# A quadratic for part of the exponentials, a tighter guard, a factor moved into a copy, and a new order

## The chip, the cores and the metric

The kernel runs on one core of one Trainium2 chip. The core has five engines that work side by side: TensorE (PE, matrix products; its weight loads are shown as PEld), ScalarE (ACT, activations), VectorE (DVE), GpSimd (POOL) and SyncE (SP, which issues most of the DMAs). The metric is the time of one execution on the device in microseconds (us). A version is judged by the median of several runs.

## The reference

Two attention blocks with 32 heads of 32 columns each work on separate inputs of 2048 rows and 1024 columns, in bfloat16, and their outputs are joined. A is plain softmax attention over all 2048 keys. B is cut into four segments of 512 rows: in each there is causal softmax attention within the segment, mixed through a gate `g` with what a memory of the earlier segments answers.

```python
# A
qkv = (x @ wqkv).reshape(B, S, 3, H, Dh).transpose(2, 0, 3, 1, 4)
scores = einsum('bhqd,bhkd->bhqk', q, k) * Dh ** -0.5
o = einsum('bhqk,bhkd->bhqd', softmax(scores), v)
a = o.transpose(0, 2, 1, 3).reshape(B, S, D) @ wo
# B
phi = lambda t: where(t > 0, t + 1.0, exp(t))
g = sigmoid(beta).reshape(1, H, 1, 1)
for s in range(4):
    p = softmax(einsum('bhqd,bhkd->bhqk', qs, ks) * Dh ** -0.5 + mask)
    a_dot = einsum('bhqk,bhkd->bhqd', p, vs)
    a_mem = (phi(qs) @ M) / (phi(qs) @ z + 1e-6)
    outs.append(g * a_mem + (1.0 - g) * a_dot)
    M, z = M + phi(ks).T @ vs, z + sum(phi(ks))
b = concat(outs) @ wo
return concat([a, b], axis=-1)
```

The logits are small: from the reference's inputs, the largest product of A is 0.042 after scaling.

## The kernel before

**Units, sets, tiles.** The heads are taken in eight groups of four (`g` in A, `j` in B). A unit of A is one group and 256 query rows, 64 units in all; a unit of B is two groups of one segment. A set is 256 query rows against two blocks of 128 keys for four heads: four tiles of 128 x 512, one for each head. A whole unit of A is eight sets. For each set TensorE writes the scores into four banks of PSUM (line 915), ScalarE takes their exponential in two instructions of 1024 columns into the ring `P` of 20 tiles (L994), and TensorE multiplies the result with the values and with a column of ones, for the sum of the row (L1090 and L1097, "P·V" in what follows; an accumulator in one PSUM bank). At the end of a unit, `recip_rows` transposes the sums (L1115), copies the values out of the bank (`keep`, L1118), takes the reciprocal (L1125), in B multiplies it by 1-g (L1127), and transposes back (L1129); GpSimd multiplies the values by it (L1175 to L1195).

**Polynomial tiles.** The table `CUBIC` gives for every four units of A which sets hand the tile of their first head to a polynomial instead of ScalarE: 118 sets, whose first exponential is 512 columns wide instead of 1024. VectorE scales the scores into `Y` (L952), GpSimd adds a constant (L955) and multiplies (L956) into `Z`, and VectorE finishes with (Z + b)·Y into `Pc` (L957). `Y` has three buffers, `Z` and `Pc` two each.

**The guard.** The polynomial, and an exponential without a bias, hold for small logits. So for each group GpSimd squares K and Q (L1266, `sqA`, `sqB`), TensorE sums the squares (L1275), VectorE takes the maxima (L1282), spreads them with TensorE's help (`dg` L1319, then L1328, L1336), and writes a bias and a flag (L1342 to L1353): the flag is set when half the sum of the largest squared norms, scaled, is over `FREE`. Before the first exponential of a group ScalarE waits for the flag, loads it and branches to a second copy of its program, with biases, where the flag is set. There the polynomial tiles are done anew by ScalarE; the instruction that would do so, the carrier, is an exponential `CARRY` half-sets later, and P·V on the tile waits for its carrier in either copy.

**Projections** (L556: K, Q and V of later groups, output projections, the memory) are jobs that share bank 6: TensorE fills it, VectorE copies it out (L1248).

**The order** is made by a planner before the program is built. Every instruction has an assumed duration (in `dve`, `act`, `pool`: elements / rate / 1000 + fixed, in us) and a key, its place on a planned time axis that advances by 1.024/1.2 + 0.051 for each full exponential. A simulated run then picks for each engine what goes next. For TensorE, scores go when the exponentials are about to need them; the rest by rank, the lowest first: P·V by how many exponentials its tile is behind (`PV_ROOM`, `PV_T`), a job by how far its key lies ahead (`JOB_AT`, `JOB_SLOPE`) and by its due time (`DUE_AT`, `DUE_SLOPE`), with `STICK` taken off for staying in the same mode. `LEAD_A` is how long before its group's first exponential a group's K, Q and guard are due. Each engine then executes its list strictly in that order, with semaphore waits, and DMAs are issued from SP's list in the same manner.

The lines around the rank, which the change reaches through its constants:

```python
def rank(x):
    if x.pvn is not None:
        k = (x.pvn + PV_ROOM - st["opn"]) * PV_T if st["rows"] and x.need - st["opn"] > PV_HOT else -100.0
    else:
        k = JOB_AT + JOB_SLOPE * max(min(x.key - st["prog"], 20.0), -20.0)
        k = min(k, DUE_AT + DUE_SLOPE * (x.due - st["prog"]))
    if x.mode == mode:
        k -= STICK
```

## Time and profile before

| | |
|---|---|
| runs | 1124.29, 1128.17, 1129.32 us; median 1128.17 |
| profiled execution | span 1128.2 us |
| DMA | 72.77 MB, 64 GB/s on the mean |
| TensorE clock granted | 0.996 on the mean |

Busy time of the engines in five stretches, us:

| stretch, us | PE | DVE | ACT | POOL |
|---|---|---|---|---|
| 0 to 50 | 43.40 | 17.15 | 33.33 | 10.40 |
| 200 to 250 | 47.59 | 33.95 | 48.64 | 34.22 |
| 400 to 450 | 43.57 | 44.64 | 48.40 | 36.46 |
| 900 to 950 | 42.13 | 35.64 | 41.26 | 34.96 |
| 1050 to 1100 | 49.34 | 24.50 | 49.81 | 20.78 |

A group of instructions is shown as: line, engine, operation, output <- input, shapes, count | busy us, mean ns of one | idle time of the engine ahead of them, and what ended most of it. A wait is shown as: engine, line <- what released it: us in total, times, longest. A row of the timeline gives start, duration, engine, line, and in brackets the idle time before. Waits at a branch and DMA issues are not counted as busy. Releasers are inferred from semaphore events.

### The profile page before, as it was taken

To read this page: it belongs to the slowest core of one execution; us is meant where nothing else is said; L and a number is where in the kernel's file an instruction comes from. 1 tells how busy PE (TensorE), PEld (TensorE's weight loads), DVE (VectorE), ACT (ScalarE), POOL (GpSimd) and SP (SyncE) were. 2 spreads that over 40 slices of the span, in tenths; PEclk is the share of its full clock that TensorE was granted. 3 is DMA by queue.
4 is the path that set the end of the run, shared out by engine and by line. 5 is a ranking of instruction groups with operands and counts; after the bars stand their busy time and mean duration, and the time that the engine had idled before them with its cause. 6 is when DMAs were issued, how large, how long until landed. Compare 5 with 4: busy or idle time off the path is not lost.

```text
span 1128.2 us, 67476 instructions
## 1 busy us (share of the span) xinstructions
PE 1045.6 (93%) x31412; PEld 724.2 (64%) x31412; DVE 744.9 (66%) x1566; ACT 1071.5 (95%) x1224; POOL 677.5 (60%) x653
## 2 busy tenths in 40 slices
PE   8989999999999988998999898988999889999998
PEld 4667666667666655666666566766667556657775
DVE  3345667756665588777865888687745868775444
ACT  4989999999999999999999999999999979999997
POOL 2215576756576576856565786775755758665431
PEclk9999999999999999999999999999999989999999
DMA  9032350005223240033241330133040640022101
GB/s 203 7 85 46 83 130 15 16 19 121 54 56 88 64 104 13 16 72 63 65 90 59 82 59 11 33 87 85 27 101 28 200 111 3 23 69 76 39 23 54
DMA packets 171145, 72.77 MB, mean 64 GB/s; under 512 B 134768, under 2 KB 169072, under 8 KB 170864
## 3 DMA queue, kind: packets, MB, share of 16 engines
q1 hardware_dynamic: 168496, 67.66, 24.8%
q8 instruction: 246, 4.03, 1.5%
q10 hardware_dynamic: 2368, 0.79, 0.3%
q14 instruction: 35, 0.29, 0.1%
HBM read 45.23 MB, written 11.67 MB: 50 GB/s over the span
## 4 chain that ended last, share of the span: by engine, by line
ACT 48%; PE 35%; DVE 8%; issue 4%; POOL 2%; SPq 1%; DMA 1%; ACTq 0%; DVEq 0%; POOLq 0%
ACT P L994 47%; PE ps L556 17%; PE ps L915 7%; PE ps L1090 5%; PE ps L1097 5%; DVE PKQ_B L1546 1%; DVE Y L952 1%; DVE Pc L957 1%; SPq L1232 1%; PE ps L1495 1%; POOL Z L955 1%; ACT PKQ_B L1541 1%; DVE T L1115 1%; POOL Z L956 1%; DVE rc L1127 1%
## 5 line engine op out<-in xcount | busy, mean ns | idle before, releaser
L994 ACT ACTIVATE P<-ps 128x1024 bf16<-128x1024 f32 (+1 forms) x1176 | 1043.1, 1076 | 35.0 <-PE ps L1097 12.9
L1097 PE MATMUL ps<-P,onesb 128*32 128x256 bf16 (+1 forms) x4628 | 297.7, 271 | 1.0 <-issue 1.0
L955 POOL TENSOR_SCALAR Z<-Y 128x512 f32<-128x512 f32 x118 | 182.2, 1544 | 158.1 <-DVE Y L952 157.5
L1090 PE MATMUL ps<-P,V_A 128*32 128x256 bf16 x3860 | 254.9, 275 | 6.1 <-ACT P L994 2.1
L915 PE MATMUL ps<-KQ_A 32*128 32x256 bf16 x4096 | 205.2, 273 | 28.7 <-ACT P L994 18.9
L956 POOL TENSOR_TENSOR Z<-Z,Y 128x512 f32<-128x512 f32 x118 | 153.1, 1297 | 4.3
L915 PEld LDWEIGHTS ps<-KQ_A 32*128 32x128 bf16 x4096 | 61.9, 92 | 141.5 <-ACT P L994 100.9
L556 PE MATMUL ps<-xT_B,W_B 128*32 128x256 bf16 x4096 | 139.5, 275 | 6.1 <-issue 1.9
L556 PE MATMUL ps<-xT_A,W_A 128*32 128x256 bf16 (+1 forms) x3968 | 138.4, 277 | 5.3 <-DMA xT_A<-in_A_x_dram 1.6
L1097 PEld LDWEIGHTS ps<-P,onesb 128*32 128x32 bf16 x4628 | 130.3, 97 | 16.5 <-issue 12.1
L1014 POOL TENSOR_SCALAR_AFFINE_SELECT P<-P 128x768 bf16<-128x768 bf16 (+1 forms) x96 | 78.6, 823 | 90.7 <-ACT P L994 86.8
L1090 PEld LDWEIGHTS ps<-P,V_A 128*32 128x32 bf16 x3860 | 109.2, 96 | 32.3 <-issue 15.9
L952 DVE TENSOR_SCALAR Y<-ps 128x512 f32<-128x512 f32 x118 | 80.9, 686 | 72.3 <-PE ps L915 71.1
L1266 POOL TENSOR_TENSOR sqA<-KQ_A 128x512 bf16<-128x512 bf16 x61 | 66.6, 1094 | 96.9 <-DVE KQ_A L1248 57.2
L556 PEld LDWEIGHTS ps<-xT_B,W_B 128*32 128x32 bf16 x4096 | 100.5, 97 | 31.3 <-issue 24.1
L556 PEld LDWEIGHTS ps<-xT_A,W_A 128*32 128x32 bf16 x3968 | 97.5, 96 | 31.6 <-issue 17.0
L957 DVE SCALAR_TENSOR_TENSOR Pc<-Z,Y 128x512 bf16<-128x512 f32 x118 | 103.3, 876 | 18.9 <-POOL Z L956 18.5
L1266 POOL TENSOR_TENSOR sqB<-KQ_B 128x512 bf16<-128x512 bf16 x64 | 69.9, 1095 | 56.6 <-DVE KQ_B L1248 40.8
L1115 DVE STREAM_TRANSPOSE T<-ps 128x256 f32<-128x256 f32 (+1 forms) x148 | 71.9, 486 | 22.9 <-PE ps L1097 17.1
L1248 DVE CAST KQ_A<-ps 128x512 bf16<-128x512 f32 x60 | 41.2, 687 | 54.0 <-PE ps L556 53.7
L556 PE MATMUL ps<-Wv_B,xT_B 128*32 128x256 bf16 x2048 | 69.8, 274 | 4.8 <-DVE V_B L1248 1.4
L1129 DVE STREAM_TRANSPOSE T<-rc 128x256 f32<-128x256 f32 (+1 forms) x152 | 72.1, 478 | 2.5
(104 smaller groups left out, 1405.8 us busy)
## 6 DMA issues: line engine op xcount, KB each, us to landing
Wv_B<-in_B_wv_dram SPq DMA_DIRECT2D x32, 256.0 KB, 3.3
W_B<-in_B_wk_dram SPq DMA_DIRECT2D x32, 256.0 KB, 3.2
W_B<-in_B_wq_dram SPq DMA_DIRECT2D x32, 256.0 KB, 4.5
Wo_B<-in_B_wo_dram SPq DMA_DIRECT2D x32, 256.0 KB, 3.3
out_dram<-outsb SPq DMA_DIRECT2D x56, 128.0 KB, 1.8
W_A<-in_A_wqkv_dram SPq DMA_DIRECT2D x14, 256.0 KB, 3.6
ot_a_scratch<-OTst SPq DMA_DIRECT2D x50, 64.0 KB, 2.2
xT_A<-ot_a_scratch SPq DMA_DIRECT2D x6, 512.0 KB, 6.7
```

The costliest lines, as they stand in the source:

```text
L556: ins = e.matmul(out[r], w[:, r], x, start=start, stop=stop, tile_position=(0, 32 * t), skip_group_check=True)
L915: ins = e.matmul(out, kap, qap, start=st, stop=True, tile_position=(32 * h, 0), skip_group_check=True)
L952: o = self.dve(lambda e: e.tensor_scalar(Y[:, :], src, KAPPA * SCALE, -KAPPA * ROOT, ALU.mult, ALU.add), 512, key - 9.0, [self.bank[bank]] ...
L955: self.pool(lambda e: e.tensor_scalar(Z[:, :], Y[:, :], CUBE_A, None, ALU.add), 512, key - BCK, [rY], [rZ], rate=0.38)
L956: self.pool(lambda e: e.tensor_tensor(Z[:, :], Z[:, :], Y[:, :], ALU.mult), 512, key - BCK, [rY, rZ], [rZ], rate=0.435)
L957: last.append(self.dve(lambda e: e.scalar_tensor_tensor(out=dst, in0=Z[:, :], scalar=CUBE_B, in1=Y[:, :], op0=ALU.add, op1=ALU.mult), 512, ...
L994: a = self.act(guarded if early else lambda e: e.activation(dst, src, ACT.Exp, scale=SCALE), cols, key, rd, wr, fixed=EXP_FIXED)
L1014: self.pool(lambda e: e.affine_select(v, v, pattern=pat, compare_op=ALU.is_ge, fill=0.0, base=0, channel_multiplier=-1), 2 * nd * P, key + ...
L1090: ins = e.matmul(self.ps[32 * h:32 * h + 32, 512 * obk + q0:512 * obk + q0 + nq], v, p, start=first, stop=last, tile_position=(0, 32 * h), ...
L1097: ins = e.matmul(self.ps[32 * h:32 * h + 32, lcol + q0:lcol + q0 + nq], self.onesb[:, 0:32], p, start=False, stop=last, tile_position=(0, ...
L1115: self.dve(lambda e: e.transpose(T2[:, 0:n], src), n, nk, rsrc, [r2], fixed=0.17)
L1266: self.pool(lambda e: e.tensor_tensor(sq[:, :], src, src, ALU.mult), 512, key, [rsrc], [rs], rate=0.5)
```

## The change

The cubic in `Y` becomes a quadratic in its vertex form, C2·(y + MID)² + REST: VectorE scales and shifts, GpSimd squares (both inputs are `Y`), and GpSimd multiplies and adds into `Pc`. VectorE's last pass is gone, and P·V on `Pc` now waits for GpSimd. The guard's limit goes from 0.125 to 0.1. The factor 1-g is applied in the copy of the values instead of to the reciprocals. The code for `CHAIN`, which was 0, goes. `CUBE_PV`, `CARRY`, the last entry of `CUBIC`, the third one, and most of the planner's constants are different, so the order of all engines' lists is planned anew.

```diff
@@ -28,16 +28,17 @@
 T_RING = 3
 PHI_AT = 7.583
 EXP_FIXED = 0.051
-FREE = 0.125
+FREE = 0.1
 UP = 1.0 + 2.0 ** -7
-KAPPA, ROOT, CUBE_A, CUBE_B = 0.5501767600212002, -1.5993248390626598, -0.9857377158509045, 1.2295944671136563
-CUBIC = [[1, 3], [1, 3], [2, 4], [1, 3], [1, 3], [1, 3], [1, 3], [1, 3], [1, 3], [1, 3], [1, 3], [1, 3], [1, 3], [1, 3], [1, 3], [1, 3, 5]]
-CHAIN = 0
-CUBE_PV = 2.427
-CARRY = 7
+C0, C1, C2 = 1.00000312, 1.00124921, 0.499688252
+MID = C1 / (2.0 * C2)
+REST = C0 - C2 * MID * MID
+CUBIC = [[1, 3], [1, 3], [1, 3], [1, 3], [1, 3], [1, 3], [1, 3], [1, 3], [1, 3], [1, 3], [1, 3], [1, 3], [1, 3], [1, 3], [1, 3], [1, 4, 6]]
+CUBE_PV = 1.563
+CARRY = 5
 WHOLE = (("A", 7, 7), ("A", 7, 6))
-BCK = 8.851
-SOON = 0.388
+BCK = 6.382
+SOON = -0.051
 
 PAIR = ((6, 0), (6, 1), (6, 2), (7, 0), (7, 1), (7, 2), (6, 3), (7, 3), (6, 4), (7, 4), (6, 5), (7, 5), (6, 6), (7, 6), (6, 7),
         (7, 7))
@@ -46,8 +47,8 @@
 WARM = (15, 8)
 X_PIECES = ((0, 0, 4, 1.4, 5.0), (0, 4, 8, 4.2, 2.4), (1, 0, 4, 3.6, 3.9), (1, 4, 8, 2.9, 3.0), (2, 0, 8, 4.4, 3.0),
             (3, 0, 8, 4.9, 3.0))
-B_FIRST, B_STEP, B_GAP = 8.777, 1.325, 3.197
-B_STEP3 = 1.03
+B_FIRST, B_STEP, B_GAP = 8.777, 1.325, 3.16
+B_STEP3 = 1.029
 
 
 class Res:
@@ -148,29 +149,29 @@
 LAT = {"PE": 0.22, "ACT": 0.29, "DVE": 0.10, "POOL": 0.15, "SP": 0.1}
 SWITCH = 0.10
 WIN = 3.413
-ROW_LEAD = 0.796
+ROW_LEAD = 0.655
 AHEAD = 19.5
-HEAT = 0.666
-STICK = 2.198
+HEAT = 0.917
+STICK = 1.597
 OVER = 1.755
-PV_ROOM = 3.546
+PV_ROOM = 3.422
 PV_T = 0.844
-PV_HOT = 1.023
+PV_HOT = 1.322
 NORM_K = 8.39
-JOB_AT = -0.604
-JOB_SLOPE = 0.767
-MARGIN = 3.147
+JOB_AT = -1.233
+JOB_SLOPE = 0.629
+MARGIN = 3.142
 RXJ = 4
-RX0 = 37.688
-LEAD_A, LEAD_B, DUE_AT, DUE_SLOPE = 14.484, 8.287, 2, 1.085
+RX0 = 37.292
+LEAD_A, LEAD_B, DUE_AT, DUE_SLOPE = 16.237, 8.287, 2, 1.277
 HOLD = {}
-XR = 11.254
-XC = 0.711
+XR = 10.156
+XC = 0.833
 STEP = 1.462
-OUT3 = 55.735
+OUT3 = 55.401
 WOA_STEP = 2.224
-OUT_D = 59.313
-M_AT = 4.042
+OUT_D = 54.565
+M_AT = 5.385
 
 
 class Prog:
@@ -949,16 +950,14 @@
 
         def f(key):
             src = self.ps[:, 512 * bank:512 * bank + 512]
-            o = self.dve(lambda e: e.tensor_scalar(Y[:, :], src, KAPPA * SCALE, -KAPPA * ROOT, ALU.mult, ALU.add), 512, key - 9.0,
+            o = self.dve(lambda e: e.tensor_scalar(Y[:, :], src, SCALE, MID, ALU.mult, ALU.add), 512, key - 9.0,
                          [self.bank[bank]], [rY], fixed=0.15)
             o.urgent = True
-            self.pool(lambda e: e.tensor_scalar(Z[:, :], Y[:, :], CUBE_A, None, ALU.add), 512, key - BCK, [rY], [rZ], rate=0.38)
-            self.pool(lambda e: e.tensor_tensor(Z[:, :], Z[:, :], Y[:, :], ALU.mult), 512, key - BCK, [rY, rZ], [rZ], rate=0.435)
-            last.append(self.dve(lambda e: e.scalar_tensor_tensor(out=dst, in0=Z[:, :], scalar=CUBE_B, in1=Y[:, :], op0=ALU.add,
-                                                                  op1=ALU.mult), 512, key - BCK, [rY, rZ], [rP], fixed=0.31))
+            self.pool(lambda e: e.tensor_tensor(Z[:, :], Y[:, :], Y[:, :], ALU.mult), 512, key - BCK, [rY], [rZ], rate=0.435)
+            last.append(self.pool(lambda e: e.tensor_scalar(dst, Z[:, :], C2, REST, ALU.mult, ALU.add), 512, key - BCK, [rZ], [rP],
+                                  rate=1.1))
         self.item(T + 0.001, f)
-        return (lambda e: e.activation(dst, Y[:, :], ACT.Exp, bias=self.bias[:, 60 + bc:61 + bc], scale=1.0 / KAPPA),
-                bc, rY, rP, last, t)
+        return (lambda e: e.activation(dst, Y[:, :], ACT.Exp, bias=self.bias[:, 60 + bc:61 + bc], scale=1.0), bc, rY, rP, last, t)
 
     def plan_exp(self, take, slot, buf, T, lo=0, fix=None):
         w = take[0]["w"]
@@ -988,7 +987,7 @@
 
                 def alt(e):
 
-                    e.wait_ge(self.pg.sems["DVE"], c.count)
+                    e.wait_ge(self.pg.sems["POOL"], c.count)
                     redo(e)
                     return guarded(e)
             a = self.act(guarded if early else lambda e: e.activation(dst, src, ACT.Exp, scale=SCALE), cols, key, rd, wr,
@@ -1020,24 +1019,16 @@
 
 
         rounds = []
-        waiting = None
         for take, pv, T, cube in sets:
             at = T + 0.3
             four = list(self.sets[take[0]["set"]])
-            late = four[0] if cube else None
             for sk in {sk for sk, _ in pv}:
                 for x in self.sets[sk]:
                     x.setdefault("fixed", -1e9)
             parts = [[(x, pi) for x in self.sets[sk]] for sk, pi in pv]
-            if cube and CHAIN:
-                parts = [[(waiting, pi)] * (waiting is not None) + p[1:] for p, (_, pi) in zip(parts, pv)]
-                waiting = late
-            elif cube:
+            if cube:
                 at += CUBE_PV
             rounds.append([max([at] + [x["fixed"] + 0.001 for p in parts for x, _ in p]), take[3]["n"], parts])
-        if waiting is not None:
-            at = max(sets[-1][2] + 0.31, waiting["fixed"] + 0.001)
-            rounds.append([at, sets[-1][0][3]["n"], [[(waiting, pi)] for _, pi in pv]])
         rounds.sort(key=lambda r: r[:2])
         rest = {h: sum(x["h"] == h for r in rounds for p in r[2] for x, _ in p) for h in range(4)}
         begun = set()
@@ -1115,7 +1106,10 @@
         self.dve(lambda e: e.transpose(T2[:, 0:n], src), n, nk, rsrc, [r2], fixed=0.17)
         if keep is not None:
             rk = self.r_keep[i]
-            self.dve(lambda e: e.tensor_copy(T2[:, n:2 * n], keep), n, nk, rsrc, [rk])
+            if scale is None:
+                self.dve(lambda e: e.tensor_copy(T2[:, n:2 * n], keep), n, nk, rsrc, [rk])
+            else:
+                self.dve(lambda e: e.tensor_scalar(T2[:, n:2 * n], keep, scale, None, ALU.mult), n, nk, rsrc + [self.r_g], [rk], fixed=0.2)
         v = T2[:, 0:n].rearrange("p (b r) -> p b r", r=32)[:, :, 0:1]
         rv = rc[:, 0:nb].unsqueeze(2)
         if add is not None:
@@ -1123,8 +1117,6 @@
             self.dve(lambda e: e.reciprocal(rc[:, 0:nb], rc[:, 0:nb]), nb * 8, key, [rr], [rr])
         else:
             self.dve(lambda e: e.reciprocal(rv, v), nb * 8, key, [r2], [rr])
-        if scale is not None:
-            self.dve(lambda e: e.tensor_scalar(rc[:, 0:nb], rc[:, 0:nb], scale, None, ALU.mult), nb, key, [rr, self.r_g], [rr])
         bc = rc[:, 0:nb].unsqueeze(2).to_broadcast([P, nb, 32])
         self.dve(lambda e: e.transpose(T2[:, 0:n].rearrange("p (b r) -> p b r", r=32), bc), n, key, [rr], [r2], fixed=0.17)
         return T2, [r2] if keep is None else [r2, rk]
@@ -1346,7 +1338,7 @@
                 out=self.bias[:, bc:bc + 1], in0=raw, scalar=-FREE, in1=raw, op0=ALU.is_lt, op1=ALU.mult), 1, key + 0.4,
                 [self.r_braw], [rb], fixed=0.3)
             if bc < 2:
-                self.dve(lambda e, bc=bc: e.tensor_scalar(self.bias[:, 60 + bc:61 + bc], self.bias[:, bc:bc + 1], ROOT, None, ALU.add), 1,
+                self.dve(lambda e, bc=bc: e.tensor_scalar(self.bias[:, 60 + bc:61 + bc], self.bias[:, bc:bc + 1], -MID, None, ALU.add), 1,
                          key + 0.4, [rb], [self.r_biasr[bc]])
             nf = self.nflag
             self.nflag += 1
```

## The prediction

> **What bounds the kernel now.** I read the busy shares first, then the waits of the fullest engine, then each of its gaps with what stood in the queues at that time.
>
> ```profile
> PE 1045.6 (93%) x31412; PEld 724.2 (64%) x31412; DVE 744.9 (66%) x1566; ACT 1071.5 (95%) x1224; POOL 677.5 (60%) x653
> ```
>
> ScalarE (ACT) is busy 1071.5 of 1128.2 us, so 56.7 us is all that any change can win that leaves its work alone. VectorE and GpSimd, the two engines whose work is cut, stand idle for a third of the span and more. By form, the exponentials are:
>
> ```profile
> L994 ACT ACTIVATE P<-ps 128x1024 bf16<-128x1024 f32 x1058 | 1007.2, 1120 | 32.7 <-PE ps L1097 12.9 <-PE ps L556 8.3 <-PE ps L915 7.6
> L994 ACT ACTIVATE P<-ps 128x512 bf16<-128x512 f32 x118 | 80.9, 685 | 2.3 <-PE ps L915 2.3
> ```
>
> The 118 half-width ones are the sets that give one of their four tiles to the polynomial. The windows of ScalarE's ends, its waits, and the gap at 60 us:
>
> ```profile
> 0.00:50.00 50.00, 43.40 (x986) 25.70 (x990) 17.15 (x41) 33.33 (x38) 10.40 (x31) 1.00 0.63 118
> 1100.00:1150.00 50.00, 23.10 (x640) 14.53 (x640) 12.31 (x22) 21.52 (x25) 4.90 (x5) 0.97 0.09 31
> ```
>
> ```profile
> ACT P L994 <- PE ps L1097: 12.9, 13, 3.6
> ACT P L994 <- PE ps L915: 9.8, 20, 0.8
> ...
> ACT P L994 <- PE ps L556: 8.3, 1, 8.3
> ```
>
> ```profile
> 62.27 3.78 ACT L994 ACTIVATE P<-ps 128x1024 bf16<-128x1024 f32 x4 [3.63 <-PE ps L1097]
> 66.44 44.44 ACT L994 ACTIVATE P<-ps 128x1024 bf16<-128x1024 f32 x50 [0.39 <-PE ps L1097]
> ```
>
> In the windows' rows the fourth busy number is ScalarE. The account of 56.7: the start (50 - 33.33) 16.7; the end (28.2 - 21.52) 6.7; one wait behind a projection (L556) 8.3; waits for scores (L915) 9.8; waits for P·V work (L1097) 12.9, of which 3.63 + 0.39 = 4.0 lie in the first group, where no tile is a polynomial, and 8.9 in 11 waits later; the remaining 2.3 are gaps too short to be listed. Only 8.9 + 9.8 + 8.3 = 27.0 us lie where the changed plan works.
>
> What the 8.9 is, at its longest instance:
>
> ```profile
> 478.70 1.92 PE L556 MATMUL ps<-xT_A,W_A 128*32 128x256 bf16 x64
> ...
> 480.67 0.27 PE L1090 MATMUL ps<-Pc,V_A 128*32 128x256 bf16 x1
> ...
> 481.21 0.28 PE L1097 MATMUL ps<-P,onesb 128*32 128x256 bf16 x4
> ...
> 481.33 1.02 ACT L994 ACTIVATE P<-ps 128x1024 bf16<-128x1024 f32 x1 [2.43 <-PE ps L1097]
> ```
>
> The view gives the reading of P, not the scores, as the last releaser: the exponential lacks a place to write. P is a ring of 20 tiles, and its oldest ones come free when P·V (L1090, L1097) has read them. TensorE did a 1.92 us projection first, and the set with the polynomial tile (Pc) went just ahead of the round that freed the place. So the polynomial does reach ScalarE, through the order of P·V and not through its own duration:
>
> ```profile
> its engine sat idle before it (us, times) until:
>   POOL Z L956: 18.5, 18
>   ACT P L994: 8.4, 24
> ...
> who waited for it (us, times):
>   PEld ps L1090: 0.3, 1
>   PEld ps L556: 0.2, 1
> ```
>
> In this view of the tile Pc, P·V on it waited 24 times for an exponential and once, 0.3 us, for the polynomial's last pass. The exponential is the "carrier": the later one that would redo the tile if the guard tripped, and after which the plan lets P·V read it. The carrier is what is late, not the polynomial.
>
> The 8.3 us gap, from the timeline around 900 us:
>
> ```profile
> 893.62 1.49 POOL L955 TENSOR_SCALAR Z<-Y 128x512 f32<-128x512 f32 x1
> 894.16 0.68 DVE L1248 CAST KQ_A<-ps 128x512 bf16<-128x512 f32 x1
> 895.70 1.27 POOL L956 TENSOR_TENSOR Z<-Z,Y 128x512 f32<-128x512 f32 x1
> 896.93 1.04 POOL L1266 TENSOR_TENSOR sqA<-KQ_A 128x512 bf16<-128x512 bf16 x1
> 900.44 0.70 DVE L1319 TENSOR_SCALAR dg<-identf,cols 128x128 bf16<-128x128 f32 x1
> 902.53 1.60 PE L556 MATMUL ps<-xT_B,W_B 128*32 128x256 bf16 x52 [1.56 <-issue]
> 904.93 0.29 PE L1328 MATMUL ps<-dg,onesb 128*32 128x256 bf16 x4 [0.36 <-DVE KQ_B L1248]
> 907.55 0.15 DVE L1353 SCALAR_TENSOR_TENSOR flags<-braw,flags 128x1 int32<-128x1 f32 x1
> 908.18 5.42 ACT L994 ACTIVATE P<-ps 128x1024 bf16<-128x1024 f32 x6 [8.31 <-PE ps L556]
> ```
>
> ScalarE resumes 0.5 us after the flag of a guard is written (L1353): it stood at the guard's branch. The view names the wrong releaser, since it counts neither the branch nor its wait. The guard's chain is the last K/Q copy (ends 894.84), its square on GpSimd (not until 896.93, behind both polynomial passes), the column maxima, dg (ready 901.14), and then L1328, which stands in TensorE's order behind a projection of the other half that stood still until 902.53 (the view names no releaser; I take it for the weights' load). The chain was some 1 us too late to go ahead of that projection, and paid 8.3.
>
> **The change part by part.** The sum is made against the profiled span of 1128.2 us; the runs shown have a median of 1128.17 (1124.29 to 1129.32). A measurement of this kernel cannot tell less than about 0.5% (5.6 us) from no change.
>
> ```profile
> L957 DVE SCALAR_TENSOR_TENSOR Pc<-Z,Y 128x512 bf16<-128x512 f32 x118 | 103.3, 876 | 18.9 <-POOL Z L956 18.5
> L952 DVE TENSOR_SCALAR Y<-ps 128x512 f32<-128x512 f32 x118 | 80.9, 686 | 72.3 <-PE ps L915 71.1
> L1118 DVE COPY T<-ps 128x256 f32<-128x256 f32 x123 | 48.0, 390 | 0.0
> L1127 DVE TENSOR_SCALAR rc<-rc,gc 128x8 f32<-128x8 f32 x64 | 34.6, 547 | 0.6
> L1319 DVE TENSOR_SCALAR dg<-identf,cols 128x128 bf16<-128x128 f32 x34 | 15.0, 441 | 0.6
> ```
>
> ```profile
> L955 POOL TENSOR_SCALAR Z<-Y 128x512 f32<-128x512 f32 x118 | 182.2, 1544 | 158.1 <-DVE Y L952 157.5
> L956 POOL TENSOR_TENSOR Z<-Z,Y 128x512 f32<-128x512 f32 x118 | 153.1, 1297 | 4.3
> L1014 POOL TENSOR_SCALAR_AFFINE_SELECT P<-P 128x512 bf16<-128x512 bf16 x32 | 22.7, 712 | 16.8 <-ACT P L994 16.6
> ```
>
> *ScalarE's work: 0.* The tables of polynomial sets before and after each sum, four units to an entry and without the first four units and the two whole ones, to 118; the exponentials stay 1058 and 118.
>
> *The parabola.* VectorE loses L957: 118 x 0.876 = 103.3 us. L952 stays with other constants. GpSimd's square is a two-input pass like L956, 1.297. The second pass (multiply and add, float32 in, bfloat16 out) has no row: above, the same opcode in L955, 1.544; below, the one-input L1014 at the same width, 0.712. The plan's own cost for it is 512/1.1 + 150 = 615 ns, and the plan's costs for L955 and L956 (1497 and 1327) lie within 4% of their rows, so I take the lower end, 0.71. GpSimd then loses 118 x (1.544 - 0.712) = 98 us, or nothing at the upper end. The passes of one tile shrink from 0.686 + 1.544 + 1.297 + 0.876 = 4.40 to 2.70 us (3.53 at the upper end). On the path this is 0 either way: the carrier covers it, and without that cover the 4.40 would have shown as waits on Pc, which come to 0.3 + 0.2. The result now sits in GpSimd's queue, where it may wait for P·V to release a Pc buffer; behind it wait squares and the causal selects (L1014). Two buffers and two such sets in eight make that distance several exponentials, so I count 0.
>
> *Factor 1-g in the copy.* 64 times L1127 goes, 34.6 us; 64 copies become a multiply by a per-partition scalar: at least 0.390 as now, at most L1319's 0.441 plus its width again (128 elements of L952's 0.686/512 = 0.17), 0.61. I take 0.45: +3.8 us (0 to 14). No ScalarE wait ends on this chain: 0.
>
> *CARRY 7 to 5.* The carrier comes two exponentials earlier, and P·V of 118 sets with it: 2 x 1.120 = 2.2 us. The plan also pulls jobs forward: their rank falls by 0.63 (JOB_AT), against 0.844 per exponential of P·V's lag, which is 0.75 exponentials or 0.8 us given back. The net 1.4 us is more than the mean ring wait, 8.9/11 = 0.81, and leaves 1.0 of the 2.43; with some jitter I keep 2.5 of the 8.9: **-6.4** (0 to -8.9).
>
> *LEAD_A 14.48 to 16.24.* K, Q and guard of a group are due 1.75 plan-us earlier; the plan's exponential takes 1.024/1.2 + 0.051 = 0.904 against 1.120 measured, so 2.2 us. GpSimd's shorter second pass takes up to 0.8 off the 2.1 us for which the square queued. Together 2.2 to 3.0 against the 1 us that was missing. I leave 2 of the 8.3: **-6.3** (+0 if the other projection gets ahead again, -8.3 at best). The loads around it move little; their DMA queue order stays.
>
> *Everything else in the plan* (slopes, stickiness, slack): the score waits of 9.8 go either way by a few us; I take **-0.5**. Sum: 1128.2 - 6.4 - 6.3 - 0.5 = **1115**.
>
> TensorE's clock after that stall:
>
> ```profile
> 908.00:912.00 4.00, 2.90 (x56) 1.24 (x52) 1.97 (x4) 3.69 (x5) 1.60 (x2) 0.54 0.21 66
> 912.00:915.40 3.40, 3.40 (x68) 1.58 (x61) 2.06 (x4) 2.97 (x4) 3.05 (x4) 0.53 0.27 81
> ```
>
> The granted clock (the column after POOL) was 0.54 and 0.53 there, while ScalarE still ran 3.69 of 4.00 and 2.97 of 3.40. The Trainium skill (TensorE: Matmul & The Clock Gate, Terms and Part 1) has the clock fall to half after an idle window and prices it at the throttled time times the missing share. By that the stall's removal would be worth 7.4 x 0.46 = 3.4 us more and the sum 1112, an estimate; ScalarE's own loss in these rows is in the account already, so the sum goes by the rows.
>
> **The rivals.** *All waits of the body go*: 27.0 us off, 1101. For it, a stretch with all kinds of work in which ScalarE never stood still:
>
> ```profile
> 950.00:1000.00 50.00, 47.06 (x1433) 32.28 (x1432) 35.37 (x79) 50.00 (x59) 29.33 (x29) 1.00 0.07 23
> ```
>
> Against: jobs are pulled forward, and the score waits have no part of the change that names them.
>
> *One of the two terms only*: 1128.2 - 6.4 = 1122.
>
> *Given back*: jobs pulled forward eat the ring's 1.4 us, and the guard's L1328 again lands behind a projection. What is left is about -2: 1126. For it: engine time was cut on engines that were not the bound.
>
> *Slower: the ring fills.* P·V of the 362 sets without a polynomial (60 units of eight, less 118) gets no earlier carrier, only jobs ranked 0.63 before it. TensorE's order, at the boundaries of the A units, then puts a 1.9 us projection before the round that frees the ring, as at 478.70, in more units. At the mean wait of 0.81 us, 23 waits in place of 11 cost 12 x 0.81 = 9.7: 1138. It decides from 7 waits more (5.7 us), the guard stall unchanged. Against: two ScalarE exponentials of relief outweigh 0.75.
>
> *The change doesn't do what it says: the guard trips.* The limit on the bound of the logits falls from 0.125 to 0.1. Worked out from the reference's inputs, the largest group bound is 0.091 (0.5 x 0.177 x the largest squared norms of q and k, 1/128 added), so the plain path stays; if it tripped throughout, each polynomial tile would be redone as a half exponential, 118 x 0.685 = 81 us: 1196.
>
> *The second pass stays at 1.54*: 1115 still, since it is covered.
>
> **How the numbers follow.** Forecast 0.50 (1108 to 1121); all waits gone 0.08; one term 0.11; given back 0.17; ring fills 0.13; guard 0.01. Faster by over 0.5% means below 1122.5: forecast, all gone and most of "one term", 0.67. Within 0.5%: given back and the rest, 0.19. Slower: 0.14. The range 1104 to 1131 leaves out the slower cases and half of "all gone".
>
> **What would show it.** ScalarE's exponentials again 1058 and 118 at 1120 and 685 ns; VectorE near 611, GpSimd near 580 us (677 if the second pass is long); waits of L994 on L1097 near 6.5 instead of 12.9; no gap over 3 us at the guard of the seventh and eighth groups, and a clock of 1.00 there. Wrong is the ring term if the L1097 waits stay at 12.9 or grow; wrong is the guard term if a gap there ends again just after a flag; wrong is the whole reading if P·V on Pc now waits for GpSimd.

## The result and the profile after

The changed kernel takes 1118.51 us (median of five runs, 1115.34 to 1120.09) against 1128.17 (1124.29 to 1129.32): the ratio is 0.9925, with a 95% interval of 0.9901 to 0.9949. That is 9.7 us faster. The two profiled executions, which the accounts below use, have spans of 1116.5 and 1128.2 us, 11.7 apart.

The busy shares, from the page of the changed kernel:

```profile
PE 1037.8 (93%) x31412; PEld 727.9 (65%) x31412; DVE 624.1 (56%) x1384; ACT 1067.4 (96%) x1224; POOL 533.7 (48%) x653
```

Its groups by form (busy us and mean ns of one, then the idle time before and its releasers):

```profile
L993 ACT ACTIVATE P<-ps 128x1024 bf16<-128x1024 f32 x1058 | 1008.2, 1146 | 24.4 <-PE ps L1088 11.9 <-PE ps L916 7.2 <-PE ps L557 3.9
L956 POOL TENSOR_TENSOR Z<-Y 128x512 f32<-128x512 f32 x118 | 123.3, 1045 | 213.8 <-DVE Y L953 181.0 <-PE ps L1088 11.2 <-PE ps L557 11.1
L957 POOL TENSOR_SCALAR Pc<-Z 128x512 bf16<-128x512 f32 x118 | 74.5, 631 | 10.1 <-PE ps L557 1.8 <-POOL Z L956 1.6 <-PE ps L1088 0.7
L1112 DVE TENSOR_SCALAR T<-ps,gc 128x256 f32<-128x256 f32 x64 | 28.6, 447 | 0.0
```

The exponentials are again 1058 and 118. GpSimd's second pass, L957, takes 631 ns; the multiply with 1-g, L1112, takes 447 ns. ScalarE is now busy for 1067.4 of 1116.5 us, 49.1 us short of the span where 56.7 were missing. Its waits (total, times, longest):

```profile
ACT P L993 <- PE ps L1088: 12.3, 11, 5.3
ACT P L993 <- PE ps L916: 8.2, 9, 1.6
...
ACT P L993 <- PE ps L557: 3.9, 1, 3.9
```

The ends of its span (the fourth busy number is ScalarE) and the gaps of the first group, from the windows and the timeline of the changed kernel:

```profile
0.00:50.00 50.00, 41.71 (x970) 25.03 (x974) 16.63 (x40) 33.15 (x38) 10.42 (x31) 1.00 0.66 118
1100.00:1150.00 50.00, 11.91 (x320) 7.36 (x316) 5.35 (x10) 9.31 (x11) 0.66 (x1) 0.99 0.06 20
```

```profile
64.12 3.77 ACT L993 ACTIVATE P<-ps 128x1024 bf16<-128x1024 f32 x4 [5.32 <-PE ps L1088]
69.88 45.15 ACT L993 ACTIVATE P<-ps 128x1024 bf16<-128x1024 f32 x51 [1.99 <-PE ps L1088]
```

| ScalarE's idle time, us | before | after |
|---|---|---|
| start (50 less its busy time) | 16.7 | 16.9 |
| first group (two ring waits) | 4.0 | 7.3 |
| ring waits later | 8.9 in 11 | 12.3 - 7.3 = 5.0 in 9 |
| score waits | 9.8 in 20 | 8.2 in 9 |
| at the guard | 8.3 | 3.9 |
| end (16.5 - 9.31) | 6.7 | 7.2 |
| rest | 2.3 | 0.6 |
| sum | 56.7 | 49.1 |

The sum falls by 7.6, and ScalarE's busy time by 4.1 for the same instructions, together 11.7. A second profiled execution of the changed kernel, from the repeat further down (span 1122.5 us), has for the ring and the scores:

```profile
ACT P L993 <- PE ps L1088: 13.9, 11, 6.8
ACT P L993 <- PE ps L916: 11.2, 17, 1.6
```

In it the first group lost 8.8 us, the later ring waits 5.1, and the guard 3.8. So the rows for the later ring waits and the guard come again, while the score waits of one kernel differ by 3 us between executions, and their fall from 9.8 to 8.2 is no more than that.

Read by these rows, the change looks like two repaired waits of the order, at the guard and in the ring. The view of the chain that ended last says something else. Before:

```profile
ACT 48%; PE 35%; DVE 8%; issue 4%; POOL 2%; SPq 1%; DMA 1%; ACTq 0%; DVEq 0%; POOLq 0%
ACT P L994 47%; PE ps L556 17%; PE ps L915 7%; PE ps L1090 5%; PE ps L1097 5%; DVE PKQ_B L1546 1%; DVE Y L952 1%; DVE Pc L957 1%; SPq L1232 1%; PE ps L1495 1%; POOL Z L955 1%; ACT PKQ_B L1541 1%; DVE T L1115 1%; POOL Z L956 1%; DVE rc L1127 1%
```

After:

```profile
ACT 57%; PE 33%; DVE 4%; issue 3%; POOL 1%; SPq 1%; DMA 1%; ACTq 0%; DVEq 0%
ACT P L993 55%; PE ps L557 17%; PE ps L916 6%; PE ps L1081 5%; PE ps L1088 4%; ACT PKQ_B L1533 1%; SPq L1224 1%; DMA xT_A<-in_A_x_dram 1%; DVE T L1106 1%; POOL P L1013 1%; ACT P L980 0%; DVE Y L953 0%; DVE KQ_A L1240 0%; DVE PKQ_B L1538 0%; PE ps L1487 0%
```

VectorE's share of the chain falls from 8% to 4%, some 90 to 45 us. The old chain holds the three later passes of the polynomial by name (L957, L955, L956) and L1127, each at a rounded 1%. In the new one neither GpSimd's passes nor the multiply is listed, and `Y` (L953) is at 0%. The first experiments ask which reading holds.

### The profile page after: what moved, and what is told of

The parts are those of the page before. It is cut to its first block, busy times and chain, and to the rows that moved or that the text cites. A ratio compares the mean times of both kernels' runs of the same rounds, so it can differ in the third digit from the quotient of the medians.

```text
span 1116.5 us, 67428 instructions
## 1 busy us (share of the span) xinstructions
PE 1037.8 (93%) x31412; PEld 727.9 (65%) x31412; DVE 624.1 (56%) x1384; ACT 1067.4 (96%) x1224; POOL 533.7 (48%) x653
## 3 DMA queue, kind: packets, MB, share of 16 engines
q8 instruction: 246, 4.03, 1.5%
## 4 chain that ended last, share of the span: by engine, by line
ACT 57%; PE 33%; DVE 4%; issue 3%; POOL 1%; SPq 1%; DMA 1%; ACTq 0%; DVEq 0%
ACT P L993 55%; PE ps L557 17%; PE ps L916 6%; PE ps L1081 5%; PE ps L1088 4%; ACT PKQ_B L1533 1%; SPq L1224 1%; DMA xT_A<-in_A_x_dram 1%; DVE T L1106 1%; POOL P L1013 1%; ACT P L980 0%; DVE Y L953 0%; DVE KQ_A L1240 0%; DVE PKQ_B L1538 0%; PE ps L1487 0%
## 5 line engine op out<-in xcount | busy, mean ns | idle before, releaser
L993 ACT ACTIVATE P<-ps 128x1024 bf16<-128x1024 f32 (+1 forms) x1176 | 1039.9, 1104 | 26.2 <-PE ps L1088 12.3
L956 POOL TENSOR_TENSOR Z<-Y 128x512 f32<-128x512 f32 x118 | 123.3, 1045 | 213.8 <-DVE Y L953 181.0
L557 PE MATMUL ps<-xT_A,W_A 128*32 128x256 bf16 (+1 forms) x3968 | 138.7, 277 | 7.8 <-DMA xT_A<-in_A_x_dram 3.6
L557 PE MATMUL ps<-xT_B,W_B 128*32 128x256 bf16 x4096 | 139.6, 276 | 4.8 <-DVE KQ_B L1240 1.9
L953 DVE TENSOR_SCALAR Y<-ps 128x512 f32<-128x512 f32 x118 | 81.5, 691 | 88.6 <-PE ps L916 84.0
L1081 PEld LDWEIGHTS ps<-P,V_A 128*32 128x32 bf16 x3860 | 109.0, 97 | 29.1 <-issue 13.9
L1258 POOL TENSOR_TENSOR sqA<-KQ_A 128x512 bf16<-128x512 bf16 x61 | 64.1, 1051 | 124.7 <-DVE KQ_A L1240 103.2
L557 PEld LDWEIGHTS ps<-xT_B,W_B 128*32 128x32 bf16 x4096 | 101.9, 97 | 27.9 <-issue 20.7
L557 PEld LDWEIGHTS ps<-xT_A,W_A 128*32 128x32 bf16 x3968 | 97.0, 96 | 34.2 <-issue 18.1
L1240 DVE CAST outsb<-ps 128x512 bf16<-128x512 f32 x56 | 38.6, 689 | 87.1 <-PE ps L557 51.1
L1240 DVE CAST KQ_B<-ps 128x512 bf16<-128x512 f32 x64 | 44.0, 688 | 71.5 <-PE ps L557 71.3
L957 POOL TENSOR_SCALAR Pc<-Z 128x512 bf16<-128x512 f32 x118 | 74.5, 631 | 10.1 <-PE ps L557 1.8
L1240 DVE CAST KQ_A<-ps 128x512 bf16<-128x512 f32 x60 | 41.3, 688 | 59.8 <-PE ps L557 59.6
L1121 DVE STREAM_TRANSPOSE T<-rc 128x256 f32<-128x256 f32 (+1 forms) x152 | 72.0, 478 | 2.6
```

The source lines that it names most:

```text
L557: ins = e.matmul(out[r], w[:, r], x, start=start, stop=stop, tile_position=(0, 32 * t), skip_group_check=True)
L953: o = self.dve(lambda e: e.tensor_scalar(Y[:, :], src, SCALE, MID, ALU.mult, ALU.add), 512, key - 9.0, [self.bank[bank]], [rY], fixed=0.15)
L956: self.pool(lambda e: e.tensor_tensor(Z[:, :], Y[:, :], Y[:, :], ALU.mult), 512, key - BCK, [rY], [rZ], rate=0.435)
L957: last.append(self.pool(lambda e: e.tensor_scalar(dst, Z[:, :], C2, REST, ALU.mult, ALU.add), 512, key - BCK, [rZ], [rP], rate=1.1))
L993: a = self.act(guarded if early else lambda e: e.activation(dst, src, ACT.Exp, scale=SCALE), cols, key, rd, wr, fixed=EXP_FIXED)
L1081: ins = e.matmul(self.ps[32 * h:32 * h + 32, 512 * obk + q0:512 * obk + q0 + nq], v, p, start=first, stop=last, tile_position=(0, 32 * h), ...
```

## The experiments

Each kernel was run beside the kernel before on the same chip; ratios are to that. Theory one, the prediction's: the passes lie beside ScalarE's work and cost nothing, and the order brings the gain. The rival: the passes' time on VectorE and GpSimd reaches the end, and shortening them brings it.

### The passes alone, in the old order

The kernel before with its planner's costs, constants and therefore every list as they were, but shorter passes in the places of the old ones:

```diff
-tensor_scalar(Z, Y, CUBE_A, None, ALU.add)                  # GpSimd
-tensor_tensor(Z, Z, Y, ALU.mult)                            # GpSimd
-scalar_tensor_tensor(dst, Z, CUBE_B, Y, ALU.add, ALU.mult)  # VectorE
+tensor_tensor(Z, Y, Y, ALU.mult)                            # GpSimd
+tensor_scalar(Z[:, 0:1], Z[:, 0:1], 1.0, None, ALU.mult)    # GpSimd, one column
+tensor_scalar(dst, Z, C2, REST, ALU.mult, ALU.add)          # VectorE
```

> The kernel before with every engine's list in its old order, but with shorter passes in each polynomial tile: the square in the place of L955, one column in the place of L956, and the multiply-add as a VectorE pass in the place of L957. Computes the parabola. GpSimd should fall to near 510 us, VectorE to near 690. Order theory: 1128, within 3 us. Relief theory: 1119 to 1122.

`Y` gets the new constants as well. Measured: 1122.77 us (1118.41 to 1125.93) beside 1129.62, ratio 0.9938 (0.9919 to 0.9957), 6.9 us faster. Its ScalarE waits:

```profile
ACT P L995 <- PE ps L1098: 13.0, 11, 3.6
...
ACT P L995 <- PE ps L558: 7.8, 1, 7.8
ACT P L995 <- PE ps L917: 4.8, 15, 0.8
```

The ring (13.0 against 12.9) and the guard (7.8 against 8.3) stay. The waits for scores halve, from 9.8 to 4.8 us, which is more than the 3 us by which two executions of the changed kernel differ. Its chain:

```profile
ACT 46%; PE 41%; DVE 6%; issue 3%; POOL 1%; SPq 1%; DMA 1%; ACTq 0%; DVEq 0%; POOLq 0%
```

Some 70% of the 9.7 us is to be had from shorter passes alone, with nothing moved. As the intervals of the two ratios overlap (0.9919 to 0.9957 here, 0.9901 to 0.9949 for the change), it may be all of it. (The load is not quite that of the change: VectorE is busy 695.3 us and GpSimd 496.2, against 624.1 and 533.7.) How, TensorE's own waits show. First the kernel before, then this one; the rows stand for the end of a unit (L1118, from then on the accumulator can be used again), and the scores' bank that `Y` reads (L952):

```profile
PE ps L1090 <- DVE T L1118: 4.0, 15, 0.4
PE ps L915 <- DVE Y L952: 3.4, 7, 1.3
```

```profile
PE ps L1091 <- DVE T L1119: 3.1, 12, 0.4
...
PE ps L917 <- DVE Y L954: 1.5, 4, 0.6
```

All rows of this view that name VectorE add up to 36.6 us in 82 waits before, and to 30.1 in 68 here. TensorE is nearly as full as ScalarE (93% against 95% before). When it waits for a bank that VectorE has yet to empty, because a pass of the polynomial is ahead in VectorE's queue, the next scores come later and ScalarE waits for those. Counted in the two traces, TensorE waited 6.3 us (16 times) before and 2.3 us (5 times) here for a VectorE instruction that followed the polynomial's last pass with no pause over 0.15 us. TensorE's account closes on the difference of the spans, 6.7 us: 6.5 less waiting for VectorE and 3.3 less busy, against 3.6 more waiting for ScalarE and DMAs (2.5 + 1.0 + 0.1 at issue), is 6.2.

### The load of the passes, put back into the new order

The changed kernel with TensorE's, ScalarE's and SP's lists untouched, and an additional pass behind `Y` on VectorE (the maximum over a constant, 809 ns, 95.5 us in all), or an additional one between the two on GpSimd (1.5 us, 178 us in all), or both:

```diff
+    tensor_reduce(cols[:, xc:xc + 5], maskbd (5 times), AX.X, ALU.max)   # VectorE, behind Y
...
+    tensor_scalar(Y, Z, 1.0, None, ALU.add)                              # GpSimd, before the last pass
```

> The changed kernel with every engine's list in the changed order, but with more work in each of the 118 polynomial tiles: one extra VectorE reduction of a constant (128 x 640) behind the first pass, and one extra GpSimd pass over the tile in the slow form of the old L955, which overwrites Y. The result is the same as long as the guard stays quiet. Load of both engines is then at or above that of the cubic (VectorE near 720 us, GpSimd near 700). Order theory (the gain comes from the planned order, engine time of the polynomial is covered): 1118.5, within 3 us. Relief theory (the gain comes from the freed VectorE and GpSimd time): back to 1126 or more.

> x3_load without its extra GpSimd pass: the changed order, and in each polynomial tile only the extra VectorE reduction (118 x 0.81 us). VectorE-release theory: most of the loss of 45 us, 1145 to 1165, with ScalarE's waits on scores near 30 us. GpSimd-queue theory: 1118 to 1126.

> x3_load without its VectorE reduction: the changed order, and in each polynomial tile only the extra slow GpSimd pass (118 x 1.51 us). VectorE-release theory (the loss of x3_load came from the VectorE pass that stands behind Y and holds up the copies that free banks and the next Y): close to the changed kernel, 1118 to 1126. GpSimd-queue theory (it came from GpSimd's queue: squares, selects and Pc late): most of the loss, 1145 to 1165.

| | median (runs), us | ratio (95%) | against the changed kernel's 0.9925 |
|---|---|---|---|
| both | 1163.98 (1155.38 to 1167.88) | 1.0317 (1.0273 to 1.0361) | +3.9%, 44 us |
| VectorE alone | 1149.78 (1148.25 to 1152.11) | 1.0201 (1.0170 to 1.0232) | +2.8%, 31 us |
| GpSimd alone | 1129.27 (1126.89 to 1131.94) | 1.0016 (1.0001 to 1.0032) | +0.9%, 10 us |

Neither load is free, though most of each is hidden, and the two nearly add up. A microsecond on VectorE costs 31/95.5 = 0.33 us of the end, one on GpSimd 10/178 = 0.06. (VectorE's busy time rises by only 696.7 - 624.1 = 72.6 us, as records of successive instructions overlap; by that it is 0.43.) With both loads VectorE is busy for 703 us and GpSimd for 712, against 745 and 678 in the kernel before, and yet the time is 34 us above that kernel's. So the new lists don't bear long passes, and the prices hold for these lists. GpSimd alone came out between the two expectations. The additional GpSimd pass also keeps its `Y` buffer longer. TensorE's waits in the changed kernel, with the additional VectorE pass, and with the additional GpSimd pass:

```profile
PE ps L1081 <- DVE T L1110: 3.2, 11, 0.4
...
PE ps L1081 <- DVE T L1112: 2.6, 9, 0.4
```

```profile
PE ps L1090 <- DVE T L1121: 9.2, 21, 1.0
PE ps L557 <- DVE KQ_B L1249: 8.5, 14, 1.2
PE ps L1090 <- DVE T L1119: 7.2, 14, 0.9
```

```profile
PE ps L1090 <- POOL Pc L958: 4.8, 6, 1.5
```

With VectorE loaded, P·V waits for the copies at a unit's end (L1121 and L1119, 16.4 us against 5.8), and projections wait for the copies of K and Q (for those of B 8.5 against 2.2). With GpSimd loaded, P·V waits for `Pc`. The rows that name VectorE add up to 29.6 us in the changed kernel and to 67.6 with the additional VectorE pass; 43.6 of the 67.6 are waits for an instruction that followed the additional pass with no such pause. The waits that name ScalarE fall by 11.0 and the others by 1.4, busy time grows by 4.0: 38.0 - 11.0 - 1.4 + 4.0 = 29.6, and the spans differ by 30.0. ScalarE sees it as late scores:

```profile
ACT P L1002 <- PE ps L916: 24.8, 53, 1.9
```

The score waits go from 8.2 (11.2 in the second execution) to 24.8 us. The chain of this run, and that of the run with the additional GpSimd pass:

```profile
PE 56%; ACT 22%; DVE 15%; issue 4%; POOL 2%; DMA 1%; DVEq 0%; ACTq 0%; POOLq 0%
```

```profile
ACT 55%; PE 31%; POOL 8%; DVE 3%; issue 2%; ACTq 0%; DVEq 0%; POOLq 0%
```

The loaded engine's share grows to 15% and to 8%, from VectorE's 4% and GpSimd's 1% in the changed kernel.

### The parabola with the old constants, the cubic with the new ones

Both replan the order. The first is the kernel before with the parabola as in the change and its costs told to the planner, every constant as before; the second is the changed kernel with the cubic's passes and costs.

```diff
-tensor_scalar(Z, Y, CUBE_A, None, ALU.add), rate=0.38
-tensor_tensor(Z, Z, Y, ALU.mult), rate=0.435
-scalar_tensor_tensor(dst, Z, CUBE_B, Y, ALU.add, ALU.mult), fixed=0.31
+tensor_tensor(Z, Y, Y, ALU.mult), rate=0.435
+tensor_scalar(dst, Z, C2, REST, ALU.mult, ALU.add), rate=1.1
...
 CARRY = 7
```

The second is the same edit backwards, with `CARRY = 5` and the new constants.

> The kernel before with the parabola of the change and its costs told to the planner, all constants of before kept (CARRY 7, LEAD_A 14.484 and the rest), so the order is planned with shorter polynomial passes only. Order theory: no gain that can be named, 1122 to 1134. Relief theory: most of the gain, 1118 to 1121.

> The changed kernel with the cubic of before (its two VectorE and two GpSimd passes, its costs told to the planner), with all constants of the change. Order theory: the gain stays, 1116 to 1123. Relief theory: the gain goes, 1126 to 1134, because this constant set was planned for shorter passes.

The first took 1135.86 us (1129.70 to 1139.42), ratio 1.0057 (1.0035 to 1.0079); the second 1175.31 (1172.09 to 1176.87), ratio 1.0400 (1.0362 to 1.0438). The longest of ScalarE's waits in the first, and then in the second:

```profile
ACT P L995 <- PE ps L1098: 21.4, 18, 3.6
```

```profile
ACT P L992 <- PE ps L914: 60.1, 68, 2.8
```

Told of the shorter passes, the planner made a list in which the ring waits grew from 12.9 to 21.4, and the kernel came out 13 us slower than with the old list kept. With the cubic under the new constants ScalarE waits 60.1 us for scores. Both are slower than either theory expected. So passes and constants belong together, and neither comparison prices the parabola by itself, since each rearranges all lists.

### CARRY and LEAD_A taken back

```diff
-CARRY = 5
+CARRY = 7
...
-LEAD_A = 16.237
+LEAD_A = 14.484
```

> The changed kernel with CARRY 7 in place of 5, all else as changed; the order is planned anew by that. Ring theory (the prediction's term): ScalarE's waits on P.V (line 1088) after the first group rise from 5.0 to 9 us or more, the time by 4 to 8 us, to 1122 to 1127. If the carrier doesn't matter: those waits stay near 5, and the time moves only by what another order brings, either way.

> The changed kernel with LEAD_A 14.484 in place of 16.237; the order is planned anew by that. Guard theory (the prediction's term): the gap at the flag of the seventh or eighth group grows from 3.9 to 6 to 9 us, the time by 2 to 5 us, to 1120 to 1124. If the gap has other causes: it stays near 4.

> The changed kernel itself, beside ot_again: 1118.5 by all theories; it gives the pair on one chip.

The changed kernel, run once more with these, took 1123.45 us (1120.22 to 1126.01) on this chip, ratio 0.9940 (0.9917 to 0.9963). CARRY back at 7: 1150.81 (1146.73 to 1152.35), 27 more. LEAD_A back at 14.484: 1136.61 (1134.91 to 1140.92), 13 more. ScalarE's waits with CARRY 7, then two with the old LEAD_A:

```profile
ACT P L993 <- PE ps L1088: 34.1, 27, 5.2
ACT P L993 <- PE ps L557: 10.9, 1, 10.9
```

```profile
ACT PKQ_B L1533 <- DVE KQ_B L1240: 10.0, 1, 10.0
...
ACT P L993 <- PE ps L557: 6.2, 1, 6.2
```

With CARRY 7 the ring waits are 34.1 us in place of 13.9 in the run beside it, so the term acts on the wait that the prediction named. The gap at the guard also grew to 10.9 although LEAD_A was left alone. With the old LEAD_A the guard's gap is 6.2, and 10.0 more are lost shortly before on a copy of B's K and Q (L1240). Both directions are as predicted, but both times are far above what was expected: the sizes are those of a new list, not of a term alone. The ring waits rise with the old LEAD_A too, to 18.5 us, where `CARRY` is untouched. All four kernels that got one part exchanged and a list planned anew are slower than the kernel they came from, by 6 to 54 us. That a constant taken back costs time therefore doesn't show by itself that this constant brought the gain.

### The loads at the guard

What is left of the guard's gap, from the timeline of the changed kernel:

```profile
893.04 0.28 PE L1320 MATMUL ps<-dg,onesb 128*32 128x256 bf16 x1
...
894.31 0.29 PE L1320 MATMUL ps<-dg,onesb 128*32 128x256 bf16 x3 [0.99 <-issue]
...
895.21 3.56 PE L557 MATMUL ps<-xT_B,W_B 128*32 128x256 bf16 x64 [0.61 <-DVE cols L1328]
...
896.33 1.94 ACT L993 ACTIVATE P<-ps 128x1024 bf16<-128x1024 f32 x2 [3.88 <-PE ps L557]
```

The guard's product (L1320) now goes ahead of the other half's projection (L557), as LEAD_A was expected to bring about. But TensorE stood still for 0.99 us after the first of its four matmuls, for nothing that the view names. All four read the same two tiles, so a late operand is no explanation. At that time six loads of 512 KB, issued together at 886.09 (L1650), filled the DMA engines. The window of the changed kernel (after POOL come the clock, the share of the DMA engines and GB/s):

```profile
892.00:896.00 4.00, 2.25 (x52) 1.45 (x44) 2.50 (x11) 0.45 (x1) 0.00 (x0) 0.90 1.02 399
```

Two kernels spread the six loads, in the changed and in the old order; SP's list alone differs.

```diff
-             lat=4.0)
+             lat=4.0, gate=True)
...
-        self.item(t7 - 5.0 + 0.1 * j, lambda key, j=j: self.load_OT(j, key))
+        self.item(t7 + 1.0 + 2.5 * j, lambda key, j=j: self.load_OT(j, key))
```

> The changed kernel with the six 512 KB loads of A's outputs (line 1650) released one after the other, each by a later exponential, instead of all at once at 886 us; the lists of the four compute engines are the same, only SyncE's differs. DMA theory (TensorE's stops without a named releaser at 893 us, and with them the wait at the guard, come from the full DMA queues, which also bring its instructions): the gap of 3.88 us ahead of the seventh group's flag shrinks to under 1.5 us and the time falls by 2 to 4 us. Order theory (the guard is late in TensorE's order): gap and time as before, 1118.5 within 1.5.

> The kernel before with the same spacing of the six loads; the lists of the four compute engines are the same as in the kernel before. DMA theory: the gap of 8.31 us shrinks by 3 us or more, time 1121 to 1125. Order theory, the one of the prediction (the guard's L1328 stands behind a projection): the gap stays near 8, 1128.

> ot_after again, beside the changed kernel on one chip. DMA theory: 1.5 to 3 us under after_again. Order theory: within 1 us of it.

In the changed order: 1116.57 us (1113.42 to 1118.15), ratio 0.9904 (0.9875 to 0.9934), and on another chip 1121.59 (1120.24 to 1124.17), ratio 0.9923 (0.9898 to 0.9947). Each is 1.9 us below the changed kernel (1118.51, and 1123.45 beside it). That is the lowest time of the study, but the runs overlap, and 0.2% is less than one comparison can tell. The same window and ScalarE's row at the guard in the first:

```profile
892.00:896.00 4.00, 3.46 (x109) 2.32 (x104) 3.05 (x7) 3.83 (x5) 2.13 (x3) 1.00 0.39 96
```

```profile
892.17 13.92 ACT L993 ACTIVATE P<-ps 128x1024 bf16<-128x1024 f32 x16 [2.62 <-PE ps L557]
```

TensorE's unnamed stop is gone, the gap is 2.6 us, not under 1.5 as the DMA theory had it, and the clock, 0.90 in the changed kernel, is 1.00. The pair on the other chip repeats it: the gaps are 3.8 and 2.6 us, and the guard's product stops in the changed kernel (first two rows) and not with the loads spread (last row).

```profile
899.61 0.28 PE L1320 MATMUL ps<-dg,onesb 128*32 128x256 bf16 x1
900.82 0.29 PE L1320 MATMUL ps<-dg,onesb 128*32 128x256 bf16 x3 [0.93 <-issue]
```

```profile
898.67 0.29 PE L1320 MATMUL ps<-dg,onesb 128*32 128x256 bf16 x4
```

The Trainium skill (TensorE: Matmul & The Clock Gate, Terms and Part 1) ties a clock of one half to an idle window of TensorE. The rows here don't decide on it: in the 4 us around the stop TensorE was busy for 2.25 us at a clock of 0.90 in the first execution of the changed kernel, and for 2.32 us at 1.00 in the second.

The traces say more on what TensorE lacked. The page of the changed kernel lists a DMA queue of its own for instructions (packets, MB, share of the DMA engines):

```profile
q8 instruction: 246, 4.03, 1.5%
```

Its 4.03 MB come to 64 bytes for each of TensorE's 62824 matmuls and weight loads. In the 14 traces TensorE stopped 103 times for 0.3 us or more with no releaser named, and 102 of these stops ended 1.2 to 1.7 us after one of the 16 KB packets of this queue had landed, though the packets come only every 4.5 us or so; by chance about one in nine would fall there. So these stops look like waits for the next instructions. No run changes that supply alone, and why a packet comes late isn't shown: full DMA engines aren't needed for it, as the kernel before stops for 0.73 us at 359.76 us with the engines 4% busy. With the loads spread, a stop of 0.78 us stands at 904.8 us, beside the loads that now run there, and ScalarE stays busy through it.

The old order took 1126.68 (1123.58 to 1130.68), ratio 0.9990 (0.9971 to 1.0008): no difference that can be told. The same window of the kernel before, and of this one:

```profile
900.00:904.00 4.00, 2.44 (x84) 1.79 (x80) 1.10 (x2) 0.00 (x0) 2.05 (x3) 1.00 1.08 366
```

```profile
900.00:904.00 4.00, 3.64 (x112) 2.52 (x104) 2.40 (x5) 0.40 (x1) 2.60 (x4) 1.00 0.43 120
```

Its timeline at the guard, where ScalarE resumes at 906.99 after 6.58 us:

```profile
903.74 0.29 PE L1328 MATMUL ps<-dg,onesb 128*32 128x256 bf16 x4 [0.36 <-DVE KQ_B L1248]
```

TensorE is busy for 3.64 of these 4 us in place of 2.44, yet of the gap of 8.3 us 6.6 remain: L1328 is still behind the projection, waiting for the copy that empties the bank (L1248). So in this pair of executions the old gap was 6.6 us of order and 1.7 of the stop beside full DMAs.

## Why the prediction was right, and where it was wrong

**The time** was forecast at 1115 (own range 1108 to 1121) and came out at 1118.5, faster by more than can be mistaken for no change. The mechanism was only in part the predicted one: the guard and the later ring waits shrank as foretold, but the passes, put at 0, are worth most of the gain or all of it in the old order, and the new order loses 44 us when they are loaded again. In the changed kernel's own account their gain stands in no row of its own, since all lists moved. What the new order adds to the shorter passes isn't shown: the repeat of the changed kernel came out at 0.9940, the short passes in the old order at 0.9938.

**The step that failed** is "On the path this is 0 either way: the carrier covers it". It was read from who waits for `Pc`: P·V waited 0.3 us once. That is right and answers another question. A pass has two effects, when its result is ready and how long it keeps its engine. The first was covered; the second delayed `Y`, the copies at units' ends and the copies of projections that stand behind it, and through the banks TensorE. The old order with shorter passes is worth 6.9 us, where the prediction had 0; the rival sentence "engine time was cut on engines that were not the bound" falls with it. The rates of the added load don't carry back to that list: by them its 49.6 us less of VectorE (744.9 - 695.3) and 181.3 less of GpSimd (677.5 - 496.2) would be worth 16 (21 by VectorE's busy time) + 10 us. They were measured on load that is added to a list made for less of it; that this is the reason isn't shown. The profile had shown the way: the chain that ended last named the passes.

**Factor 1-g.** The copy takes 447 ns (taken: 450), and 34.6 us of L1127 are gone. The forecast gave 0 for it by the same argument, which no longer stands. It wasn't run alone; its share is open.

**CARRY.** Forecast -6.4 in the ring; the later ring waits fell by 3.9, and the first group, which the prediction left out, rose by 3.3. The run with 7 agrees with the sign, with the reservation above. A premise was off: 1.120 us was taken for the pitch of the exponentials, but it is the mean length of instructions that overlap. 1058 of them keep ScalarE busy for 1007.2 us before, 0.952 each, so two are 1.9 us and not 2.2. LEAD_A's 1.75 plan-us were stretched by the same figure: by 0.952 they are 1.8 us and not 2.2.

**LEAD_A.** Forecast -6.3 with 2 us left of the gap; measured -4.4 with 3.9 left. The late chain was read rightly, and the product now precedes the projection. What was mis-sized is the rest: 1.3 us of it is TensorE's stop beside the loads. "I take it for the weights' load" was a guess about the same kind of stop before; that stop went with the burst spread, but in the changed kernel it fell inside four matmuls on the same operands, so a late operand is no explanation. The timing of the packets points to its instructions. The clock was forecast at 1.00 and was 0.90 and 0.68 in two windows of 4 us; in the second execution it was 1.00, with a gap of 3.8 us all the same.

**Everything else.** -0.5 forecast; score waits -1.6 (+1.4 in the second execution), rest of the gaps -1.7, ScalarE busy -4.1. The last has no cause shown.

**The rivals.** "The guard trips" is out: the exponentials are the same in number. "The ring fills" didn't come, but stood close: the parabola under the old constants shows it (21.4 us). "The second pass stays at 1.54" is out, with 631 ns: less than the lower bound of 712.

**What would show it.** VectorE was to be near 611 us (624.1) and GpSimd near 580 (533.7: the square of one tensor takes 1045 ns, not L956's 1297, and the second pass 631 and not 712). Waits of L993 on the ring were to be near 6.5 and are 12.3. P·V never waits for `Pc` in the changed kernel; the sentence on what would show "the whole reading" wrong looked in the wrong place.

## What to carry to other kernels

Whether work is hidden is a question about the queue and not only about its result: look who stands behind it on its engine, whether the chain that ended last names it, and load the engine once with a dummy pass in an unchanged order to get the price of its microsecond. Here, with VectorE at 56 to 66% busy, a microsecond added to it still cost a third of one or more. When a planner makes the order, a comparison with one constant changed compares two lists; keep the lists and change durations if the price of an operation is wanted.

## What was not expected of the hardware

**A pass of GpSimd depends much on its form.** At 128x512 the one-operation add from float32 to float32 takes 1501 ns as the additional pass (1544 in the cubic), the multiply-and-add from float32 to bfloat16 only 631 (L957 of the changed kernel). The square with one tensor as both inputs takes 1045, the product of two tensors 1297. Why isn't shown; type, operation and output tensor differ together.

**Some of VectorE's operations stretch while GpSimd works.** Minimum, median and maximum of two lines of the kernel before, from the view of one line's instructions:

```profile
L957 DVE SCALAR_TENSOR_TENSOR Pc<-Z,Y x118: 622/752/1524, 89.0 to 1104.5; 128x512 bf16<-128x512 f32 x118
```

```profile
L1127 DVE TENSOR_SCALAR rc<-rc,gc x64: 190/532/1249, 166.2 to 1017.3; 128x8 f32<-128x8 f32 x64
```

Eight elements take 190 to 1249 ns (L1127). Counted in the trace, the 30 instructions of L957 with no GpSimd instruction beside them took 622 to 694 ns, the 88 others 641 to 1524. The Trainium skill (SBUF — State Buffer, SBUF: two separate sides) has the two engines share a pair of ports that one holds for a whole instruction, when VectorE's has two inputs in SBUF or runs in a two-port mode. The stretch of L957, with two inputs in SBUF, agrees. The last pass of the run with the old order and shorter passes has one and reaches 1302 ns too, from a median of 419; no run shows whether it ran in such a mode. `Y` in the changed kernel, read from PSUM, keeps to 651 to 693.

**TensorE stops with no releaser named.** At the guard it stood for 0.99 and 0.93 us in two executions of the changed kernel, and for 1.56 us in the kernel before, at 366 to 404 GB/s; with the loads spread, at 96 to 130 GB/s, these stops went. Similar ones come with quiet DMA engines (0.73 us at 4%). What they share is their time: 102 of 103 ended 1.2 to 1.7 us after a packet of the instruction queue had landed.
